# Loading turned decays, keys and queries as whole 128-row transfers, in a linear-attention and expert kernel

## The chip, the cores and the metric

The kernel runs on one core of a Trainium2 chip. The metric is the device time of one execution in microseconds, taken as the median of several runs; less is better. In the rows below, PE is the matrix engine (PEld its weight loads), DVE the vector engine, ACT the scalar engine, POOL the GpSimd engine and SP the queue that issues most transfers; L66 is the line of a helper through which every operation is recorded, so operations are told apart by their tiles.

## What is computed

Two stages. The first is a linear attention with a decaying state, over 4 batches, 8 heads, 768 steps and 48 channels:

```python
for t in range(S):
    state = alpha[:, :, t, :, None] * state + np.einsum('bhd,bhe->bhde', k[:, :, t], v[:, :, t])
    y[:, :, t] = np.einsum('bhd,bhde->bhe', q[:, :, t], state)
```

The second takes the 3072 rows of y (384 wide), picks for each row one of 8 experts by the largest gate logit, and computes `gate * (relu(x @ w1[e]) @ w2[e])` with an inner width of 1024.

## The kernel before

**Stages.** The attention works on 12 blocks (`PS`), here called pairs: a pair is 128 time steps of two batches with all 8 heads of each. Time runs along the free dimension. A head's 48 channels lie on partitions, and two heads share the 128 partitions: one on partitions 0 to 47, one on 64 to 111. Partitions 48 to 63 and 112 to 127 hold nothing that the result needs. Each of `X` (decays), `KT` and `QT` (keys, queries) holds 8 such double heads side by side (`KS = 8`), 4 of each half `z`. The host lays the inputs out in this shape with the unused rows already filled (`turned`: 1 for decays, 0 for keys and queries), so that the arrays in memory have all 128 rows.

For a pair, DVE scans the decays backward into `G` (`back`) and forward into `Fw` (`forth`), a half `z` at a time. POOL multiplies keys by `G` into `kh`; DVE or POOL multiplies queries by `Fw` into `qh`. PE forms the scores (`scores`), ACT copies them out as `scT`, POOL masks them (`causal`), PE multiplies them with the values `vt` (`from_values`) and adds the state's part (`from_state`). The finished rows `xs` are stored to memory by `store`. Pairs overlap: in step s of the loop, DVE scans pair s or s + 1 while PE handles the scores of pair s - 1.

Behind the attention the rows are routed, and 13 blocks of experts follow, in which PE multiplies almost without a pause.

**What sets the order.** Each engine keeps program order. SP issues the loads one after another: in front of the loop (lines 155 to 165) those of pair 0 in halves, those of pair 1 in halves with the values between, and the small gate weights `wgp`; in the loop the keys, queries and values of pair s + 1 at the head of step s (`load(s + 1, "kqv")`) and decays of a later pair at its end. There are 3 buffers for `X` and for `VT`, 2 for `KT` and `QT`.

**The lines that the change touches.** `load_turned` (lines 133 to 139) loads pair 0 over all 128 partitions, and every other pair as two transfers of 48 rows, one for each head of a double head. Because those transfers never write partitions 48 to 63 and 112 to 127, four ACT instructions (lines 157 to 160) fill the buffers that pair 0 does not use, once: `X[1]`, `KT[1]`, `QT[1]`, `X[2]`. Line 165 loads `wgp`.

Of the kernel before, what the change touches and what calls it, by code (L numbers as in the profile page):

```python
# [15 lines left out]
AF = mybir.ActivationFunctionType  # L16
# [5 lines left out]
P = 128  # L22
B, H, S, D = 4, 8, 768, 48
NC = S // P
NP = H // 2
SEG = P + 1
# [22 lines left out]
KS = 2 * NP  # L49
# [26 lines left out]
def attention_moe(ctx: ExitStack, tc: tile.TileContext, q, k, v, alpha, at_, kt_, qt_, vt_, mid, wg, wgp_, mb, w1, w2, out):  # L76
    nc = tc.nc
    order = [1]
    vec, act, pool, pe, sp = (Ordered(e, tc, order) for e in (nc.vector, nc.scalar, nc.gpsimd, nc.tensor, nc.sync))
# [6 lines left out]
    ident = cp.tile([P, P], F32, name="ident")  # L86
# [14 lines left out]
    NX_, NB, NV = 3, 2, 3  # L101
    KT = [ea.tile([P, KS, P], F32, name=f"kt{i}") for i in range(NB)]
    QT = [ea.tile([P, KS, P], F32, name=f"qt{i}") for i in range(NB)]
    X = [ea.tile([P, KS * SEG + 1], F32, name=f"X{i}") for i in range(NX_)]
# [25 lines left out]
    def small(p, *shape):  # L130
        return ps.tile([p, *shape], F32, name=next_bank())

    def load_turned(dst, src, s, z):
        if s == 0:
            sp.dma_start(dst[:, z], src[s, :, z])
        else:
            for g in range(2):
                r = slice(64 * g, 64 * g + D)
                sp.dma_start(dst[r, z], src[s, r, z])

    def load(s, names="akqv"):
        z = {"0": slice(0, NP), "1": slice(NP, KS)}.get(names[-1], slice(0, KS))
        for n in names:
            if n == "a":
                c = slice(z.start and z.start * SEG + 1, z.stop * SEG + 1)
                load_turned(X[s % NX_], at_, s, c)
            elif n in "kq":
                load_turned((KT if n == "k" else QT)[s % NB], kt_ if n == "k" else qt_, s, z)
            elif n == "v":
                sp.dma_start(VT[s % NV][:, : 2 * DM], vt_[s])  # L150

# [2 lines left out]
    wgp = cp.tile([P, NP, 32], F32, name="wgp")  # L154
    for n in "a0 k0 q0 a1 k1 q1".split():
        load(0, n)
    for t, x in ((X[1], 1.0), (KT[1], 0.0), (QT[1], 0.0), (X[2], 1.0)):
        n = KS * SEG + 1 if x else KS * P
        flat = t if x else t.rearrange("p k t -> p (k t)")
        act.activation(flat, ident[:, 0:1].broadcast_to([P, n]), AF.Copy, bias=x, scale=0.0)  # L160
    load(1, "a0")
    load(0, "v")
    for n in "k0 a1 q0 k1 q1 v".split():
        load(1, n)
    sp.dma_start(wgp, wgp_)


    room = ra.tile([P, 1024], F32, name="room")
# [37 lines left out]
    for i in range(2):  # L206
        t = ac.tile([P, KS, 64], F32, name=f"UB{i}")
# [55 lines left out]
    def back(s, z):  # L263
        x, G = X[s % NX_], st[s, "G"]
        r = slice(z.start * SEG + 1, z.stop * SEG + 1)
        vec.tensor_tensor_scan(G[:, r][:, ::-1], x[:, r][:, ::-1], DR[:, ::-1], 0.0, op0=ALU.mult, op1=ALU.max)

    def totals(s, z):
        r = slice(z.start * SEG + 1, z.stop * SEG + 1)
        vec.reciprocal(DF[:, 0::SEG], st[s, "G"][:, r][:, 0::SEG])  # L270

    def forth(s, z):
        f = slice(z.start * SEG, z.stop * SEG)
        vec.tensor_tensor_scan(st[s, "F"][:, f], X[s % NX_][:, f], DF, 0.0, op0=ALU.mult, op1=ALU.add)

    def scaled_keys(s, z, engine):
        engine.tensor_tensor(st[s, "k"][:, z], KT[s % NB][:, z], seg(st[s, "G"][:, 1:], 1, z), op=ALU.mult)

    def scaled_queries(s, z, engine=vec):
        engine.tensor_tensor(st[s, "q"][:, z], QT[s % NB][:, z], seg(st[s, "F"], 1, z), op=ALU.mult)  # L280

    def begin(s):
        st[s, "G"] = sb.tile([P, KS * SEG + 1], F32, name="G")
        st[s, "F"] = ea.tile([P, KS * SEG], F32, name="Fw", bufs=1)
        st[s, "k"] = sb.tile([P, KS, P], F32, name="kh")
        st[s, "q"] = sb.tile([P, KS, P], F32, name="qh")
# [7 lines left out]
    def scores(s, z):  # L294
        kh, qh = st[s, "k"], st[s, "q"]
        pp = [bank(NP, P) for _ in range(2)]
        for j in range(NP):
            for g in range(2):
                r = slice(64 * g, 64 * g + D)
                pe.matmul(pp[g][:, j], kh[r, NP * z + j], qh[r, NP * z + j], start=True, stop=True)  # L300
        sc = sb.tile([P, 2, NP, P], F32, name="scT", bufs=3)
        for g in range(2):
            act.copy(sc[:, g], pp[g])
        st[s, "s", z] = sc
        causal(s, z)
# [10 lines left out]
    def turn_keys(s, z):  # L316
        if z == 0:
            st[s, "n"] = sb.tile([P, 2, NP, P], F32, name="knat", bufs=1)
        p = bank(NP, P)
        for j in range(NP):  # L320
            pe.transpose(p[:, j], st[s, "k"][:, NP * z + j], ident)
        act.copy(st[s, "n"][:, z], p)
# [49 lines left out]
    def state(s):  # L372
        if s % NC > 0:
            S1 = sb.tile([P, KS, D], F32, name="S")
            kv = st[s - 1, "kv"]
            if s % NC > 1:
                vec.tensor_tensor(S1, UB[(s - 1) % 2][:, :, :D], kv, op=ALU.add)
            else:
                vec.tensor_copy(S1, kv)
            st[s, "S"] = S1  # L380
# [16 lines left out]
    def outputs(s, zs=(0, 1)):  # L397
        if 0 in zs:
            st[s, "yt"] = sb.tile([P, 2, NP, P], F32, name="yt")
        for z in zs:  # L400
            act.copy(st[s, "yt"][:, z], st[s, "yp"][z])
# [552 lines left out]
    def warm(n):  # L954
        w = bank(NP, P)
        for i in range(n):
            pe.matmul(w[:, i % NP], ident, ident, start=True, stop=True)

    for s in range(PS):
        if 0 < s and s + 1 < PS:  # L960
            load(s + 1, "kqv")
        if 0 <= s - 2:
            outputs(s - 2)
        late, by = [], vec
        if s == 0:
            warm(14)
            begin(0)
            for z in ZS:
                back(0, z)
                scaled_keys(0, z, pool)  # L970
                totals(0, z)
                forth(0, z)
                scaled_queries(0, z, pool if z == Z0 else vec)
        elif s == 1:
            begin(1)
            scores(0, 0)
            for z in range(2):
                turn_keys(0, z)
                if z == 0:
                    warm(2)  # L980
            back(1, Z0)
            scaled_keys(1, Z0, pool)
            scores(0, 1)
            totals(1, Z0)
            forth(1, Z0)
            scaled_queries(1, Z0, pool)
            back(1, Z1)
            scaled_keys(1, Z1, pool)
            totals(1, Z1)
            forth(1, Z1)  # L990
            scaled_queries(1, Z1)
        else:
            if (s - 1, "S") not in st:
                state(s - 1)
            decayed(s - 1)
            run(s, "state")
            for z in range(2):
                scores(s - 1, z)
            run(s, "masks")
            todo = scans(s)  # L1000
            if len(todo) > 1:
                late = todo.pop()
            if s >= 4:
                by = pool
            for f in todo:
                do(f)
            run(s, "counts")
        if 1 < s:
            keys(s - 1)
        if 0 <= s - 2:  # L1010
            rows(s - 2)
        if 0 <= 2 * (s - 3) < TURNED:
            turn_logits(s - 3)
        if 0 <= s - 2:
            logits_turned(s - 2)
        run(s, "small")
        if 0 <= 2 * (s - 3) < TURNED:
            sum_logits(s - 3)
        run(s, "middle")
        do(late[:-1])  # L1020
        if 0 <= s - 1:
            from_state(s - 1)
        if 0 <= s - 1 and (s - 1) % NC == 0:
            states(s - 1)
        if TURNED <= 2 * (s - 2):
            add_logits(s - 2)
        if 0 <= s - 1 and (s - 1) % NC:
            states(s - 1)
        run(s, "sums")
        for f, *x in late[-1:]:  # L1030
            f(*x, by)
        if 0 <= s - 1:
            from_values(s - 1)
        run(s, "end")
        for c in range(s - (s < 5), s + 1 - (s < 4)):
            if 0 <= c < PS:
                guard(c)
        if 0 <= s - 2:
            store(s - 2)
        for c in range(s + 2 + (s > 4), s + 3 + (s > 3)):  # L1040
            if c < PS:
                load(c, "a")
        if s == 1:
            sp.dma_start(mi.rearrange("p t w -> p (t w)"), mid.bitcast(I32))
            sp.dma_start(mbb, mb.unsqueeze(0).broadcast_to([P, NM, E]))
        if s == 2:
            sp.dma_start(xd[MID : MID + 1], of[0:1])
            sp.dma_start(gd[MID : MID + 1], of[0:1, 0:1])
# [54 lines left out]
    t = GROUPS[-2:]  # L1103
# [204 lines left out]
    for u in range(2):  # L1308
        us = slice(u * P, (u + 1) * P)
        op = py.tile([P, 512], F32, name=f"y{u}")[:, :DM]  # L1310
        for f in range(NF):
            j, z = divmod(f, 2)
# [110 lines left out]
```

## Time and profile before

| what | value |
|---|---|
| median of 3 runs | 348.19 us (347.65 to 348.42) |
| the profiled execution | 347.23 us |
| its span, first to last instruction | 345.5 us |
| PE busy | 334.1 us, 97% |
| DVE busy | 267.2 us, 77% |
| ACT busy | 234.3 us, 68% |
| POOL busy | 170.3 us, 49% |
| moved by DMA | 75.74 MB, mean 219 GB/s |

The profile is of one execution. Its own time is 1.73 us more than its span. A busy share is an average over stages with different limits, so it doesn't tell what a change in one stage is worth; the windows and timelines of that stage do. In a timeline, the bracket at a row's end is the time that the engine stood idle before it and what ended that time.

### The profile page before, as it was taken

What the parts mean: (1) busy time and instruction counts of PE and PEld (TensorE: products, weight loads), DVE (VectorE), ACT (ScalarE), POOL (GpSimd) and SP (SyncE); (2) the same over time, 40 slices, a digit from 0 to 9 for tenths busy, and PEclk for the clock granted to TensorE, in tenths of its full rate; (3) what the DMA queues carried; (4) which work ended last, traced back from release to release, by engine and by line L of the source; (5) the groups of instructions that cost most, each with busy time, mean ns of one, the idle gap of its engine ahead of it and who ended that gap; (6) DMA issues with size and microseconds to landing.
All of it is one profiled execution on the core that took longest, in us unless ns stands there. A gap on an engine that the chain in (4) does not pass through costs nothing. (4 is left out here: it accounts for less than half of the span.)

```text
span 345.5 us, 8427 instructions
## 1 busy us (share of the span) xinstructions
PE 334.1 (97%) x3162; PEld 303.7 (88%) x3162; DVE 267.2 (77%) x487; ACT 234.3 (68%) x458; POOL 170.3 (49%) x185
## 2 busy tenths in 40 slices
PE   8898999999999999999999999999999999999992
PEld 8787888888888886898989898989898989898992
DVE  7969999999995868786868686969696969696630
ACT  6766787767686524777777777777676767676540
POOL 8767689789668126556352424241254342411031
PEclk9998999999999999999999999999999999999997
DMA  7899999999455893998767667676586777670001
GB/s 236 234 235 276 289 222 237 249 258 260 140 183 187 290 341 84 367 383 283 260 217 237 242 208 246 208 250 207 188 259 232 230 243 210 244 224 25 2 25 56
DMA packets 39224, 75.74 MB, mean 219 GB/s; under 512 B 4443, under 2 KB 20980, under 8 KB 39172
## 3 DMA queue, kind: packets, MB, share of 16 engines
q1 hardware_dynamic: 35076, 65.05, 62.6%
q0 software_dynamic: 4096, 10.05, 8.7%
q8 instruction: 27, 0.44, 0.6%
q14 instruction: 25, 0.20, 0.2%
HBM read 65.43 MB, written 9.65 MB: 217 GB/s over the span
## 5 line engine op out<-in xcount | busy, mean ns | idle before, releaser
L66 PE MATMUL b<-xHL,w1H 128*128 128x512 f32 (+1 forms) x312 | 102.6, 378 | 0.5 <-ACT yt L66 0.5
L66 POOL DMA_INDIRECT out_dram<-os,idx x25 | 27.5, 1099 | 110.3 <-ACT os L66 65.3
L66 PE MATMUL b<-xHL,w1L 128*128 128x256 f32 x288 | 80.6, 280 | 0.0
L66 PEld LDWEIGHTS b<-xHL,w1H 128*128 128x128 f32 x312 | 57.4, 188 | 11.9 <-ACT yt L66 0.6
L66 PE MATMUL y<-w2H,hH 128*128 128x384 f32 x184 | 62.6, 340 | 0.0
L66 PE MATMUL y<-w2H,hL 128*128 128x384 f32 x184 | 61.7, 335 | 0.0
L66 PE MATMUL y<-w2L,hH 128*128 128x384 f32 x184 | 61.6, 335 | 0.0
L66 DVE TENSOR_TENSOR hs<-b,low 128x256 f32<-128x256 f32 x88 | 33.9, 414 | 32.7 <-ACT low L66 28.7
L66 PEld LDWEIGHTS b<-xHL,w1L 128*128 128x128 f32 x288 | 54.2, 188 | 0.1
L66 DVE TENSOR_TENSOR w1L<-w1r,w1H 128x768 fp32r<-128x768 f32 x48 | 43.8, 951 | 6.3 <-ACT w1H L66 6.3
L66 DVE TENSOR_TENSOR w2L<-w2r,w2H 128x768 fp32r<-128x768 f32 x48 | 45.8, 958 | 3.4 <-ACT w2H L66 3.4
L66 ACT ACTIVATE os<-y,gg 128x384 f32<-128x384 f32 x25 | 14.6, 584 | 39.6 <-PE y L66 37.5
L66 ACT CAST w2H<-w2r 128x768 fp32r<-128x768 f32 x48 | 40.1, 842 | 0.0
L66 ACT COPY low<-b 128x256 f32<-128x256 f32 x88 | 30.1, 368 | 14.5 <-PE b L66 13.0
L66 POOL DMA_INDIRECT xg<-xd,idx x26 | 29.6, 1138 | 20.8 <-DVE idx L66 11.6
L66 ACT CAST w1H<-w1r 128x768 fp32r<-128x768 f32 x48 | 37.9, 839 | 0.6 <-ACT ls L66 0.6
L66 POOL DMA_INDIRECT gg<-gd,idx x26 | 28.7, 1105 | 17.1 <-issue 13.4
L66 PEld LDWEIGHTS y<-w2L,hH 128*128 128x128 f32 x184 | 34.6, 188 | 0.0
L66 PEld LDWEIGHTS y<-w2H,hH 128*128 128x128 f32 x184 | 34.6, 188 | 0.0
L66 PEld LDWEIGHTS y<-w2H,hL 128*128 128x128 f32 x184 | 34.5, 188 | 0.0
L66 POOL TENSOR_TENSOR kh<-kt,G 128x512 f32<-128x512 f32 x24 | 28.8, 1206 | 10.7 <-DVE G L66 3.5
L66 ACT ACTIVATE hH<-hs 128x512 fp32r<-128x512 f32 x44 | 27.9, 634 | 7.6 <-DVE hs L66 6.1
(183 smaller groups left out, 602.7 us busy)
## 6 DMA issues: line engine op xcount, KB each, us to landing
w1r<-in_w_dram SPq DMA_DIRECT2D x26, 768.0 KB, 5.8
w2r<-in_w_dram SPq DMA_DIRECT2D x26, 768.0 KB, 5.2
vt<-in_paired_v_dram SPq DMA_DIRECT2D x12, 384.0 KB
xd<-xs SPq DMA_DIRECT2D x12, 384.0 KB, 4.6
X<-in_turned_alpha_dram SPq DMA_DIRECT2D x20, 193.7 KB, 6.3
kt<-in_turned_k_dram SPq DMA_DIRECT2D x20, 192.0 KB, 4.7
qt<-in_turned_q_dram SPq DMA_DIRECT2D x20, 192.0 KB, 7.6
kt<-in_turned_k_dram SPq DMA_DIRECT2D x2, 256.0 KB
```

The costliest lines, as they stand in the source:

```text
L66: ins = f(*a, **kw)
```

## The change

Every load of decays, keys and queries becomes one transfer over all 128 partitions, the unused rows included, as pair 0's already were. `load_turned` goes. The four fills on ACT go, since each load now writes the unused rows too. The load of `wgp` moves from the front of the loop to the end of step 0, behind the load of pair 2's decays.

```diff
-    def load_turned(dst, src, s, z):
-        if s == 0:
-            sp.dma_start(dst[:, z], src[s, :, z])
-        else:
-            for g in range(2):
-                r = slice(64 * g, 64 * g + D)
-                sp.dma_start(dst[r, z], src[s, r, z])
-
     def load(s, names="akqv"):
         z = {"0": slice(0, NP), "1": slice(NP, KS)}.get(names[-1], slice(0, KS))
         for n in names:
             if n == "a":
                 c = slice(z.start and z.start * SEG + 1, z.stop * SEG + 1)
-                load_turned(X[s % NX_], at_, s, c)
+                sp.dma_start(X[s % NX_][:, c], at_[s, :, c])
             elif n in "kq":
-                load_turned((KT if n == "k" else QT)[s % NB], kt_ if n == "k" else qt_, s, z)
+                sp.dma_start((KT if n == "k" else QT)[s % NB][:, z], (kt_ if n == "k" else qt_)[s, :, z])
             elif n == "v":
                 sp.dma_start(VT[s % NV][:, : 2 * DM], vt_[s])
...
     for n in "a0 k0 q0 a1 k1 q1".split():
         load(0, n)
-    for t, x in ((X[1], 1.0), (KT[1], 0.0), (QT[1], 0.0), (X[2], 1.0)):
-        n = KS * SEG + 1 if x else KS * P
-        flat = t if x else t.rearrange("p k t -> p (k t)")
-        act.activation(flat, ident[:, 0:1].broadcast_to([P, n]), AF.Copy, bias=x, scale=0.0)
     load(1, "a0")
     load(0, "v")
     for n in "k0 a1 q0 k1 q1 v".split():
         load(1, n)
-    sp.dma_start(wgp, wgp_)
...
             if c < PS:
                 load(c, "a")
+        if s == 0:
+            sp.dma_start(wgp, wgp_)
         if s == 1:
```

How this moves SP's instructions at the start of the program, as one piece of the difference (`X_86` to `X_88` are the three buffers of the decays, `kt_` and `qt_` those of keys and queries, `vt_` the values; the last number is the row length in words):

```order
-L66 DMA X_87<-in_turned_alpha_dram 48x517 x2
+L66 DMA X_87<-in_turned_alpha_dram 128x517
 L66 DMA vt_89<-in_paired_v_dram 128x768
-L66 DMA kt_83<-in_turned_k_dram 48x512 x2
-L66 DMA X_87<-in_turned_alpha_dram 48x516 x2
-L66 DMA qt_85<-in_turned_q_dram 48x512 x2
-L66 DMA kt_83<-in_turned_k_dram 48x512 x2
-L66 DMA qt_85<-in_turned_q_dram 48x512 x2
+L66 DMA kt_83<-in_turned_k_dram 128x512
+L66 DMA X_87<-in_turned_alpha_dram 128x516
+L66 DMA qt_85<-in_turned_q_dram 128x512
+L66 DMA kt_83<-in_turned_k_dram 128x512
```

Two transfers of 48 rows become one of 128 in the same place; nothing else changes its place there but `wgp`.

SP's next instructions in before, with the semaphores that each waits for (`DMAHW0` to `DMAHW7` are eight semaphores that transfers use in turn, so a transfer waits for the eighth one before it to land; the other names are engines that release a buffer):

```order
L66 DMA vt_90<-in_paired_v_dram 128x768 [waits DMAHW3_49]
L66 DMA wgp<-in_wgp_dram 128x128 [waits DMAHW4_49]
L66 DMA X_88<-in_turned_alpha_dram 48x1033 [waits DMAHW5_49,Activation_49]
L66 DMA X_88<-in_turned_alpha_dram 48x1033 [waits DMAHW6_49]
L66 DMA kt_82<-in_turned_k_dram 48x1024 [waits DMAHW7_49,Pool_49]
L66 DMA kt_82<-in_turned_k_dram 48x1024 [waits DMAHW0_49]
L66 DMA qt_84<-in_turned_q_dram 48x1024 [waits DMAHW1_49,DVE_49]
L66 DMA qt_84<-in_turned_q_dram 48x1024 [waits DMAHW2_49]
```

and the same place in the changed kernel:

```order
L66 DMA vt_90<-in_paired_v_dram 128x768 [waits DMAHW5_49]
L66 DMA X_88<-in_turned_alpha_dram 128x1033 [waits DMAHW6_49]
L66 DMA wgp<-in_wgp_dram 128x128 [waits DMAHW7_49]
L66 DMA kt_82<-in_turned_k_dram 128x1024 [waits DMAHW0_49,Pool_49]
L66 DMA qt_84<-in_turned_q_dram 128x1024 [waits DMAHW1_49,DVE_49]
```

The load of pair 2's decays stands ahead of `wgp` now and no longer waits for ACT's fill; all of SP's instructions until the program's end go from 640 to 604. On ACT the four fills are gone from the head of the queue; PE, DVE and POOL have the same instructions in the same order.

## Rows read from the trace of the kernel before

**Rows 1.** The page's head and its line of busy times, whole program.

```profile
span 345.5 us, 8427 instructions
...
PE 334.1 (97%) x3162; PEld 303.7 (88%) x3162; DVE 267.2 (77%) x487; ACT 234.3 (68%) x458; POOL 170.3 (49%) x185
```

**Rows 2.** Windows: length; busy PE, PEld, DVE, ACT, POOL; granted clock, DMA share, GB/s.

```profile
28.00:29.00 1.00, 1.00 (x9) 0.78 (x8) 0.93 (x3) 0.39 (x1) 1.00 (x2) 0.50 1.01 264
50.00:60.00 10.00, 10.00 (x202) 8.74 (x194) 9.38 (x14) 7.46 (x17) 10.00 (x10) 1.00 1.05 233
```

**Rows 3.** Timeline of PE, 12 to 60 us: start, length, operation, [idle before].

```profile
14.09 1.09 PE L66 MATMUL b<-scT,vt 128*64 128x128 f32 x16 [0.84 <-POOL scT L66]
...
17.03 1.16 PE L66 MATMUL b<-qh,kh 48*128 48x128 f32 x16 [0.63 <-DVE qh L66]
...
20.02 0.64 PE L66 MATMUL b<-yt,wgp 128*32 128x256 f32 x8
...
24.45 1.16 PE L66 MATMUL b<-qh,kh 48*128 48x128 f32 x16
27.01 1.57 PE L66 MATMUL b<-qh,kh 48*128 48x128 f32 x16 [1.39 <-DVE qh L66]
...
36.26 2.06 PE L66 MATMUL b<-qh,kh 48*128 48x128 f32 x32
...
44.83 2.06 PE L66 MATMUL b<-qh,kh 48*128 48x128 f32 x32
```

**Rows 4.** Timeline of POOL, 11 to 36 us.

```profile
11.79 1.19 POOL L66 TENSOR_TENSOR kh<-kt,G 128x512 f32<-128x512 f32 x1 [0.84 <-DMA kt<-in_turned_k_dram]
12.95 1.09 POOL L66 TENSOR_SCALAR_AFFINE_SELECT scT<-scT 128x1024 f32<-128x1024 f32 x1
...
15.16 1.18 POOL L66 TENSOR_TENSOR kh<-kt,G 128x512 f32<-128x512 f32 x1
...
32.44 2.35 POOL L66 TENSOR_TENSOR kh<-kt,G 128x512 f32<-128x512 f32 x2
```

**Rows 5.** Timeline of DVE, 14 to 36 us.

```profile
15.46 1.42 DVE L66 TENSOR_TENSOR qh<-qt,Fw 128x512 f32<-128x512 f32 x1 [0.18 <-DMA qt<-in_turned_q_dram]
...
19.27 1.23 DVE L66 TENSOR_TENSOR_SCAN G<-X,room 128x516 f32<-128x516 f32 x1 [1.92 <-DMA X<-in_turned_alpha_dram]
...
22.82 0.69 DVE L66 TENSOR_TENSOR qh<-qt,Fw 128x512 f32<-128x512 f32 x1 [0.77 <-DMA qt<-in_turned_q_dram]
...
26.17 0.69 DVE L66 TENSOR_TENSOR qh<-qt,Fw 128x512 f32<-128x512 f32 x1
...
34.95 0.69 DVE L66 TENSOR_TENSOR qh<-qt,Fw 128x512 f32<-128x512 f32 x1
```

**Rows 6.** Windows (columns as in rows 2), read for the last two columns.

```profile
2.00:6.00 4.00, 4.00 (x20) 4.00 (x20) 3.16 (x8) 3.99 (x5) 3.63 (x15) 1.00 0.98 303
11.00:12.00 1.00, 1.00 (x32) 0.88 (x30) 0.86 (x3) 0.70 (x2) 0.21 (x1) 1.00 0.81 201
57.00:58.00 1.00, 1.00 (x36) 0.81 (x32) 1.00 (x2) 1.00 (x4) 1.00 (x2) 1.00 1.07 197
62.00:63.00 1.00, 1.00 (x12) 0.89 (x9) 0.93 (x3) 1.00 (x3) 0.55 (x1) 1.00 1.11 416
150.00:160.00 10.00, 10.00 (x59) 9.50 (x59) 5.99 (x9) 6.05 (x11) 3.73 (x4) 1.00 1.05 386
```

**Rows 7.** The page's DMA issues: count, KB of each, us to landing.

```profile
vt<-in_paired_v_dram SPq DMA_DIRECT2D x12, 384.0 KB
...
X<-in_turned_alpha_dram SPq DMA_DIRECT2D x20, 193.7 KB, 6.3
kt<-in_turned_k_dram SPq DMA_DIRECT2D x20, 192.0 KB, 4.7
```

**Rows 8.** Timeline of ACT, 1 to 13 us.

```profile
8.68 1.07 ACT L66 COPY scT<-b 128x512 f32<-128x512 f32 x2 [2.67 <-PE b L66]
...
11.30 1.07 ACT L66 COPY scT<-b 128x512 f32<-128x512 f32 x2 [0.56 <-PE b L66]
```

## The prediction

> **What bounds the kernel now.** I read the page's busy line first, then the windows, then the timelines of PE, DVE and POOL where PE stands still, then the DMA rate of single stretches. PE is busy 334.1 us of a span of 345.5 us [rows 1]. From the fourth pair on it does not pause: between 50 and 60 us it is busy for all 10.00 us, DVE for 9.38 us [rows 2], and the scores of two neighbouring pairs start at 36.26 and 44.83 us with no idle time noted in between, 8.57 us a pair [rows 3]. A microsecond in the attention loop is therefore worth something only if it lets PE start that unbroken run earlier, or run it faster.
>
> Ahead of the run PE stands still at three places [rows 3]: 0.84 us before 14.09 (for POOL's masked scores), 0.63 us before 17.03 (for a query product on DVE) and 1.39 us before 27.01 (for a query product on DVE). [...] From the second half of one pair's scores to the first half of the next takes 36.26 - 27.01 = 9.25 us there. [...]
>
> Two of the three halts lead back to a transfer. Before 14.09: POOL waited 0.84 us for `kt`, then did `kh` (1.19 us) and only then the mask [rows 4]. Before 27.01: DVE waited 1.92 us for `X` at 19.27 and 0.77 us for `qt` at 22.82, and ran without a further wait up to the query product at 26.17 [rows 5].
>
> The transfers are late because the DMA engines are full (share 1.05 from 50 to 60 us [rows 2]) at a low rate: 197 GB/s where the 48-row loads pass, against 416 GB/s between them and 386 GB/s in the weight loads [rows 6].
>
> **The change, part by part.**
>
> *Bytes and rate.* Six 48-row loads of a pair, 2 x (193.7 + 192 + 192) = 1155 KB [rows 7], become three of 128 rows: 516.5 + 512 + 512 = 1540.5 KB, a third more. `vt` (384 KB [rows 7]) and the store of `xs` (384 KB by its shape) stay. In before, 1.18 MB at 197 GB/s take 6.0 us and the other 0.79 MB at 386 GB/s 2.0 us: 8.0 us of a PE step of 8.57 us. No 128-row load with rows of 4 KB is in the trace. Bounds: 197 GB/s, if long rows are what is slow; 416 GB/s, the best stretch. I take 386, since the 48-row loads are slow with short rows too: the first ones, with 2 KB rows, show 201 GB/s at a share of 0.81 from 11 to 12 us, so 248 at a full one, against 303 for the 128-row loads of 2 KB rows from 2 to 6 us [rows 6]. Then 1.58 MB take 4.1 us, and the step's transfers 6.1 us. The DMA engines stop being full.
>
> *Is X of pair 2 on time?* The queue ahead of it, and with it, holds 1540.5 KB each of pairs 0 and 1, two `vt` of 384 KB and its own 516.5 KB: 4365.5 KB, 4.47 MB. At 303 GB/s, the mean of the first loads (128 rows throughout) from 2 to 6 us [rows 6], it ends at 2.0 + 14.8 = 16.8 us; at 386 GB/s at 13.6. DVE could begin at 17.35 (19.27 - 1.92). It comes in time at both ends. DVE's chain from there to the query product's end is 26.86 - 19.27 - 0.77 = 6.82 us, so it is ready at 24.2 or earlier; PE arrives at 25.0 (below). X may land 0.8 us late before PE sees it.
>
> *`kt` of pair 1, first half*: 2.50 MB with what stands ahead; at 303 GB/s 10.2 us, at 386 8.5 us. POOL is free for it at 11.79 - 0.84 = 10.95 us [rows 4]. The mask behind can't start before ACT has copied the scores, 11.30 + 1.07 = 12.37 us [rows 8], so it gains 12.95 - 12.38 = 0.57 us at most, and does so if `kt` lands by 11.2 us.
>
> *The halts.* Mask 0.57 us earlier: PE's 14.09 becomes 13.52. All of POOL's queue behind moves with it, so the next `kh` (15.16 to 16.34) ends at 15.77. The query product at 15.46 lasts 1.42 us, against 0.69 us for the same operation at 22.82 and 26.17 [rows 5]; it runs beside that `kh` and ends 0.54 us after it [rows 4, 5]. If it stays behind `kh`, it ends 0.57 us earlier; if it were free of it, at 15.28 + 0.69 = 15.97, 0.91 us earlier. I take the first, by the row. [...] So PE's 17.03 becomes 16.46, the halt before it as long as it was, and PE reaches the end of the next half scores (24.45 + 1.16 = 25.61) at 25.04. The query product is there at 24.2, so the 1.39 us go whole. Sum: 0.57 + 1.39 = **1.96 us**.
>
> *The clock.* With those 1.39 us gone no pause is left right ahead of the slow stretch. The halts of 0.84 and 0.63 us were not followed by a slow one. I expect the clock to stay up: **1.68 us**; the other end is 0.
>
> *What is late next.* PE would ask for the second half of pair 3's scores at 37.25 - 3.64 = 33.6. DVE's query product for it ends at 35.64 [rows 5], 2.69 us (1.92 + 0.77) earlier 32.95: in time by 0.65 us. POOL's two `kh` end at 34.79 [rows 4]; the mask ahead of them waits for ACT and so follows PE, and they end near 32.4. No new halt, but little room.
>
> *At nothing.* The four ACT fills: ACT stands idle 2.67 us behind them [rows 8]. SP issues 36 transfers fewer (640 - 604 rows of its order); each waits for the eighth one before it to land (the order rows), so those in flight hold more than twice the bytes. The 64 KB of `wgp` now stand behind X of pair 2 and are first used at 20.02 us [rows 3]; by the sum above they land near 17.0 at the slow end. If `wgp` were late, PE would wait there one for one.
>
> **Sum.** 1.96 + 1.68 = 3.64 us of the profiled execution's 347.23 us. The median of the runs is 348.19, 0.96 us above it; I set the same 3.64 off against the median: **344.6 us**.
>
> **The rivals.**
>
> 1. *The waits go, the clock still falls* (here or a little later; the start of PE's work is as ragged as before). 348.19 - 1.96 = 346.2 us. For it: 0.63 us of halt remain at 16.5. Against: the row of the half clock follows the longest halt.
>
> 2. *Long rows are slow, whatever the partitions.* Then 1.58 MB at 197 GB/s take 8.0 us, with 2.0 us for the rest 10.0 us a pair against PE's 8.57: 1.4 us for each of nine pairs, +13 us less what is gained, near 359 us. It decides from 1.58 / (8.57 - 2.0) = 240 GB/s down. For it: every 4 KB load shown is slow. Against: the 248 GB/s of the 2 KB loads of 48 rows (above). [...]
>
> 3. *Another wait takes the place.* DVE is at 9.38 of 10 us [rows 2]; if DVE or POOL can't keep the earlier pace (the 0.65 us above), PE halts at pair 3 or 4 for about what it gained: 347.6 to 348.6 us, no change.
>
> [...]
>
> **How the numbers follow.** Forecast (344.6) 0.48; rival 1 0.27; rival 3 0.12; rival 2 and other losses, such as `kt` or `wgp` late at the start by over a microsecond, 0.06; rival 4 0.07. The range takes rivals 1 and 4 in, and half a microsecond on either side of them for the step from one execution to a median: 343.3 to 347.2. A measurement of this kernel tells about 0.2%, 0.7 us, from no change. Faster than 347.5: 0.48 + 0.27 + 0.07 and a little of rival 3, 0.84; same 0.10; slower 0.06.
>
> **What would show it.** Right: no wait of DVE for `X` and of POOL for `kt` in the list of waits; DMA share of a late attention window near 0.75, with no 197 GB/s stretch; PE without idle time from about 16.5 us; pair 3's scores (now 36.26) at about 32.6 with the clock full, 34.3 with the slow stretch. Wrong: 197 GB/s stretches that stay, new waits of PE for DVE or POOL between 25 and 45 us, or a span shorter by less than the shift of pair 3's scores, which would mean that the stage of the experts gives it back.

## The result and the profile after

The changed kernel takes **343.96 us** (median of 6 runs, 343.68 to 344.31). The kernel before, on the same chip, takes 348.56 us (6 runs, 347.65 to 351.53). The ratio is 0.9853, 95% interval 0.9815 to 0.9891. (Ratios here leave out runs more than 1.5% above the fastest of their kernel, and need not be the quotients of the medians.) The forecast was 344.6 us with a range of 343.3 to 347.2. The two profiled executions differ less than the medians: 347.23 before, 343.79 after, so 3.44 us.

The page of the changed kernel, its head and its line of busy times, against [rows 1]: the span is 3.4 us shorter, and PE's busy time fell by 3.3 us. PE does the same 3162 multiplications; it runs none of them at the half clock now (granted 1.00 in every stretch from 0 to 338 us; before, 0.50 from 28 to 31 us), which is worth 1.61 to 1.68 us (below), about half of the 3.3 us. In a second profiled execution of each kernel PE's busy time fell by 1.5 us (333.8 to 332.3). ACT has lost its four fills (458 instructions became 454).

```profile
span 342.1 us, 8364 instructions
...
PE 330.8 (97%) x3162; PEld 300.7 (88%) x3162; DVE 265.7 (78%) x487; ACT 229.5 (67%) x454; POOL 170.8 (50%) x185
```

The timeline of PE in the changed kernel, with the operations of [rows 3]:

```profile
13.90 1.09 PE L66 MATMUL b<-scT,vt 128*64 128x128 f32 x16 [0.34 <-POOL scT L66]
15.06 1.16 PE L66 MATMUL b<-qh,kh 48*128 48x128 f32 x16
16.84 1.16 PE L66 MATMUL b<-qh,kh 48*128 48x128 f32 x16 [0.62 <-DVE qh L66]
...
24.27 2.06 PE L66 MATMUL b<-qh,kh 48*128 48x128 f32 x32
...
32.84 2.06 PE L66 MATMUL b<-qh,kh 48*128 48x128 f32 x32
...
41.41 2.06 PE L66 MATMUL b<-qh,kh 48*128 48x128 f32 x32
```

The scores of pair 2 are one row now (24.27, 32 multiplications): the halt of 1.39 us between their halves is gone. Pair 3's scores start at 32.84 where they started at 36.26, so 3.42 us earlier; 32.6 was predicted. From pair 2 on a step is 8.57 us.

Windows of the changed kernel, columns as in [rows 2]; they answer to [rows 2, 6]:

```profile
11.00:12.00 1.00, 1.00 (x28) 0.88 (x25) 0.86 (x3) 0.39 (x1) 0.74 (x2) 1.00 1.04 385
28.00:29.00 1.00, 1.00 (x17) 0.42 (x16) 0.85 (x3) 1.00 (x4) 1.00 (x1) 1.00 1.03 407
50.00:60.00 10.00, 10.00 (x160) 8.84 (x159) 9.56 (x13) 8.13 (x18) 10.00 (x10) 1.00 0.93 315
57.00:58.00 1.00, 1.00 (x22) 1.00 (x21) 1.00 (x2) 0.46 (x2) 1.00 (x2) 1.00 0.83 232
```

At 28 to 29 us the granted clock is 1.00, where it was 0.50. From 11 to 12 us the transfers run at 385 GB/s instead of 201. Between 50 and 60 us the DMA engines move 315 GB/s at a share of 0.93; before it was 233 GB/s at 1.05. More bytes pass and less of the engines' time goes. The 232 GB/s from 57 to 58 us stand beside a share of 0.83, so they are partly a lack of work.

The timeline of DVE at the start, against [rows 5]:

```profile
6.86 1.23 DVE L66 TENSOR_TENSOR_SCAN G<-X,room 128x516 f32<-128x516 f32 x1 [0.71 <-DMA X<-in_turned_alpha_dram]
...
10.22 1.22 DVE L66 TENSOR_TENSOR_SCAN G<-X,room 128x516 f32<-128x516 f32 x1
...
15.63 1.06 DVE L66 TENSOR_TENSOR qh<-qt,Fw 128x512 f32<-128x512 f32 x1
16.62 0.55 DVE L66 COPY S<-kv 128x384 f32<-128x384 f32 x1
17.09 1.21 DVE L66 TENSOR_TENSOR_SCAN G<-X,room 128x516 f32<-128x516 f32 x1
...
23.56 0.69 DVE L66 TENSOR_TENSOR qh<-qt,Fw 128x512 f32<-128x512 f32 x1
```

And that of POOL, against [rows 4]:

```profile
11.52 1.20 POOL L66 TENSOR_TENSOR kh<-kt,G 128x512 f32<-128x512 f32 x1 [0.26 <-DVE G L66]
12.76 1.09 POOL L66 TENSOR_SCALAR_AFFINE_SELECT scT<-scT 128x1024 f32<-128x1024 f32 x1
...
14.97 1.17 POOL L66 TENSOR_TENSOR kh<-kt,G 128x512 f32<-128x512 f32 x1
```

The waits of DVE for `X` (1.92) and `qt` (0.77) and of POOL for `kt` (0.84) are gone behind pair 0. The wait for the second half of pair 0's own `X` is longer (0.71). DVE begins pair 2's scan at 17.09, 2.18 us earlier, and has the query product at 24.25; the mask of POOL is only 0.19 us earlier. SP issues pair 2's `X` at 9.10 us instead of 14.40. In the timeline of SP before:

```profile
14.40 0.84 SPq L66 DMA_DIRECT2D X<-in_turned_alpha_dram  x2
```

and after:

```profile
9.10 0.33 SPq L66 DMA_DIRECT2D X<-in_turned_alpha_dram  x1
```

So this load lands earlier for two reasons that come together: the transfers ahead of it pass faster (385 GB/s from 11 to 12 us instead of 201), and there are fewer of them to wait for (pair 1 comes in 6 loads instead of 12; with 12 loads over all 128 partitions, the column halves below, SP issues it at 12.33 us).

### The profile page after: what moved, and what is told of

It is laid out like the page before. It is cut to its first block, busy times and chain, and to the rows that moved or that the text cites. A ratio compares the mean times of both kernels' runs of the same rounds, so it can differ in the third digit from the quotient of the medians.

```text
span 342.1 us, 8364 instructions
## 1 busy us (share of the span) xinstructions
PE 330.8 (97%) x3162; PEld 300.7 (88%) x3162; DVE 265.7 (78%) x487; ACT 229.5 (67%) x454; POOL 170.8 (50%) x185
## 5 line engine op out<-in xcount | busy, mean ns | idle before, releaser
L66 DVE TENSOR_TENSOR hs<-b,low 128x256 f32<-128x256 f32 x88 | 33.9, 415 | 32.6 <-ACT low L66 32.6
L66 ACT COPY scT<-b 128x512 f32<-128x512 f32 x48 | 24.8, 599 | 14.2 <-PE b L66 13.1
L66 POOL TENSOR_TENSOR kh<-kt,G 128x512 f32<-128x512 f32 x24 | 30.5, 1278 | 6.3 <-DVE G L66 5.7
```

The costliest lines, as they stand in the source:

```text
L66: ins = f(*a, **kw)
```

## The experiments

Most of them cut the loads of pairs 1 to 11 in another way. The kernel before ran beside each batch on that batch's chip: 348.32 us median (345.02 to 350.53, 23 runs) for the first four, 347.92 (345.06 to 352.74, 26 runs) for the next four, 348.76 (345.58 to 352.11, 23 runs) for the next three. Its runs spread over 5.5 to 7.7 us; those of the changed kernel over 0.6 and, when it ran again, 2.2 us.

**All rows, but in two transfers of 64** (the changed kernel, with this for the loads of pairs 1 to 11; the rest of the edit is left out here).

```diff
+            for g in range(2):
+                r = slice(64 * g, 64 * g + 64)
+                sp.dma_start(dst[r, z], src[s, r, z])
```

> The changed kernel, but each load of pairs 1 to 11 in two transfers of 64 rows (partitions 0 to 63, then 64 to 127): the same bytes as the changed kernel, as many transfers as before. Theory A (a transfer that stays within one half of the partitions runs at half the rate): 197 GB/s in these loads, so 1.58 MB take 8.0 us and a pair's transfers 10.0 us against the 8.57 us of PE; the attention becomes bound by transfers, waits of DVE for X and POOL for kt in most pairs, and the time is 9 to 14 us longer than before, 356 to 362 us. Theory B (fewer instructions in flight, no fills, wgp moved): the number of transfers is that of before, so the gain of the transfers goes, the time is near before's, 347 to 349 us, with the 197 GB/s stretches lasting a third longer. Theory C (whole rows give the gain by their alignment or length): as fast as the changed kernel, 344 us.

Measured: 357.99 us (357.62 to 361.05, 4 runs), ratio 1.0309 (1.0247 to 1.0371). The same bytes as in the changed kernel, 14 us slower, and within the range of theory A. Its list of waits (us in total, times, longest):

```profile
DVE qh L66 <- DMA qt<-in_turned_q_dram: 8.8, 6, 2.3
POOL qh L66 <- DMA qt<-in_turned_q_dram: 5.0, 4, 1.5
POOL kh L66 <- DMA kt<-in_turned_k_dram: 3.1, 2, 2.0
```

Two rows of its PE timeline, halts that go on far into the attention:

```profile
29.83 1.16 PE L66 MATMUL b<-qh,kh 48*128 48x128 f32 x16 [2.18 <-DVE qh L66]
...
65.67 1.98 PE L66 MATMUL b<-qh,UB 64*64 64x128 f32 x32 [3.47 <-POOL UB L66]
```

Rows, their length and the bytes are those of the changed kernel; only the cut differs. So it is not the reading of unused rows that helps, nor their length that harms. The time is that of rival 2, from another cause: the DMA engines, at a share of 1.03 to 1.07 from 20 to 60 us, move 227 to 273 GB/s and can't keep up with a pair per 8.57 us.

**One transfer of 112 rows** (partitions 0 to 111, the kernel before otherwise, fills kept).

```diff
-            for g in range(2):
-                r = slice(64 * g, 64 * g + D)
-                sp.dma_start(dst[r, z], src[s, r, z])
+            r = slice(0, 64 + D)
+            sp.dma_start(dst[r, z], src[s, r, z])
```

> Before with one transfer of 112 rows (partitions 0 to 111) for each load of pairs 1 to 11, the fills kept: an eighth fewer bytes than the changed kernel, both halves of the partitions reached, as few transfers. Theory A (what counts is that one transfer reaches both halves): most of the gain, 343.8 to 345.5 us, the DMA share of a late attention window under 1. Rival (what counts is the full 128 rows, evenly spread over the DMA engines): rates near those of 48 rows, 347 us or more.

Measured: 351.12 us (346.61 to 352.51, 12 runs), ratio 1.005 (1.0009 to 1.0091): slower than before. One transfer that reaches both halves is not enough: theory A fell. Its window from 50 to 60 us shows a full DMA and a PE that is not:

```profile
50.00:60.00 10.00, 9.61 (x168) 7.75 (x166) 8.84 (x13) 7.21 (x17) 8.32 (x9) 1.00 1.03 299
```

**All 128 rows, in two transfers by columns** (the changed kernel, each load of pairs 1 to 11 cut in the free dimension; the two lines that use it are left out here).

```diff
+    def load_turned(dst, src, s, z):
+        h = (z.start or 0) + (z.stop - (z.start or 0)) // 2
+        parts = [z] if s == 0 else [slice(z.start, h), slice(h, z.stop)]
+        for c in parts:
+            sp.dma_start(dst[:, c], src[s, :, c])
```

> The changed kernel, but every load of X, kt and qt of pairs 1 to 11 is split in two by columns: each transfer still covers all 128 partitions, with rows of half the length (1 or 2 KB). Refined theory (what counts is that one transfer covers all 128 rows evenly; the run of 112 rows and the run of two times 64 rows each lack that): about the changed kernel, 343.5 to 345.5 us, 128-row stretches near 400 GB/s, no new wait of DVE for qt. Rival (what made the two times 64 rows slow was twice the number of transfers, with half the bytes in flight when each waits for the eighth ahead of it): slow like that run, 350 to 360 us, waits of DVE for qt of 2 us and more.

Measured: 344.51 us (343.24 to 346.22, 6 runs), ratio 0.9879 (0.983 to 0.9928), as the changed kernel. The rival fell. Twice the transfers cost nothing that the median shows, but something in the trace: SP issues pair 2's `X` at 12.33 us instead of 9.10, and DVE waits for it again. Its list of waits has this row, whose longest wait, 1.3 us, is that of pair 2 (the other two are pair 0's):

```profile
DVE G L66 <- DMA X<-in_turned_alpha_dram: 3.2, 3, 1.3
```

PE does not halt for it, and pair 3's scores start at 33.79 us instead of 32.84. What these three runs leave standing is that for the gain every transfer here has to cover all 128 partitions; fewer transfers bring the first loads sooner, which by itself is worth less than the runs can tell.

The page's DMA queues say the same in bytes and engine time. The hardware queue of the kernel before (packets, MB, share of the 16 engines' span):

```profile
q1 hardware_dynamic: 35076, 65.05, 62.6%
```

Of the changed kernel:

```profile
q1 hardware_dynamic: 35652, 69.38, 58.8%
```

Of the run with two times 64 rows:

```profile
q1 hardware_dynamic: 36228, 69.38, 64.8%
```

Of the run with 112 rows:

```profile
q1 hardware_dynamic: 35076, 67.21, 62.0%
```

Of the run with column halves:

```profile
q1 hardware_dynamic: 40836, 69.38, 60.0%
```

Share times span (345.5, 342.1, 355.9, 349.3, 342.5 us) is 216, 201, 231, 217 and 206 us of all 16 engines, so 301, 345, 301, 310 and 338 GB/s while they work, with the same weights among the bytes in all. The changed kernel moves 4.3 MB more in 15 us less.

So two transfers, one on each half of the partitions, bring 301 GB/s and one of 112 rows 310, where transfers over all 128 bring 338 and 345. No view here shows which engine writes which rows, so why the two halves and the 112 rows are slow stays open.

**Only X, or only kt and qt, as 128 rows** (the kernel before otherwise).

```diff
-        if s == 0:
+        if s == 0 or dst.shape[1] == KS * SEG + 1:
```

> The kernel before, with only X loaded over 128 partitions in one transfer; kt and qt stay two times 48 rows. Proportional theory (each narrow load takes the DMA engines' time, and the gain is in the sum): 516.5 + 768 KB at 386 GB/s and 768 KB at 197 GB/s make 3.4 + 4.0 = 7.4 us of a pair's 8.57, against 8.0 before and 6.1 after, so a third of the gain: 346 to 347.5 us. Rival (X of pair 2, the longest wait of DVE, is what matters, and it is now one wide load): 344 to 345.5 us, no wait of DVE for X behind pair 1.

> The kernel before, with only kt and qt loaded over 128 partitions in one transfer each; X stays two times 48 rows. Proportional theory: 1024 + 768 KB at 386 GB/s and 387 KB at 197 GB/s make 4.75 + 2.0 = 6.75 us of a pair's 8.57, two thirds of the gain or more: 344 to 345.5 us. Rival (X of pair 2 is what matters, and it is still narrow): 346 to 347.5 us, with a wait of DVE for X of a microsecond or more ahead of pair 2.

Measured: X alone 349.35 us (345.56 to 351.04, 12 runs), ratio 0.9994 (0.9953 to 1.0036), no gain; kt and qt alone (the test is `KS` then) 346.22 us (344.69 to 349.04, 12 runs), ratio 0.9958 (0.992 to 0.9996), some 2.5 us of medians. By the ratio the gain of kt and qt alone is 0.4%, some 1.5 us, with an interval that ends just short of no change. The rival (X of pair 2 alone matters) fell. The proportional theory has the order right and both sizes too good. The profiled execution with X alone is the slowest of its twelve (351.04 us), so it is read for its single waits only. DVE waits for `X` of pair 2 in spite of the wide load, and longer than before for `qt`:

```profile
DVE G L66 <- DMA X<-in_turned_alpha_dram: 3.1, 3, 1.4
DVE qh L66 <- DMA qt<-in_turned_q_dram: 1.4, 1, 1.4
```

The longest wait for `X` is pair 2's. Together the two waits of pair 2 are 1.41 + 1.37 = 2.78 us, where they were 1.92 + 0.77 = 2.69 [rows 5]. That the narrow `kt` and `qt` around it hold up a wide `X`, because they share the DMA engines, fits but is not shown. In the trace with kt and qt alone DVE waits 0.57 us for pair 2's `X` and not for `qt`, and PE's third halt is gone.

**Only pairs 1 and 2, or only pairs 3 to 11, as 128 rows** (the condition `s == 0` becomes `s <= 2`, or `s == 0 or s > 2`).

> Before, with the loads of pairs 1 and 2 alone as 128-row transfers; fills and wgp as in before, pairs 3 to 11 in two of 48 rows. Theory A (all of the gain comes from pairs 1 and 2 being on time and the clock that stays up): within 0.8 us of the changed kernel, 343.7 to 344.8 us, PE's first scores of pair 3 near 32.8 us, no half clock, while 197 GB/s stretches stay in the later pairs. Rival (the relief of the transfers in all pairs matters): clearly above, 346 us or more, with new waits for X, kt or qt of pairs 3 and 4.

> Before, with pairs 3 to 11 as 128-row transfers and pairs 1 and 2 in two of 48 rows as before. Theory A: the halts of PE before 14.09, 17.03 and 27.01 us stay, and so does the slow clock behind them where it comes: 347.5 to 349 us, no change from before that can be told, though the DMA share of a late attention window falls from 1.05 to 0.9. Rival (all pairs): faster than before by 1 us or more.

Measured: the early pairs alone 344.53 us (343.35 to 346.66, 6 runs), ratio 0.9887 (0.9846 to 0.9928); the late pairs alone 346.55 us (343.58 to 348.13, 12 runs), ratio 0.9972 (0.9937 to 1.0007). Nearly the whole gain is made by the loads of two pairs, ahead of PE's unbroken run, as the prediction's reading had it. The late pairs' interval takes in no change, but the median lies 1.8 us lower (1.0 us by the ratio), lower than I had expected of them: that is left unexplained, and a gain of a microsecond from the later loads is not ruled out. Pair 3's scores in the profiled executions, first of the early pairs alone (346.66 us, the slowest of its six), then of the late pairs alone (343.58, the fastest of its twelve):

```profile
33.30 2.32 PE L66 MATMUL b<-qh,kh 48*128 48x128 f32 x32
```

```profile
33.82 2.06 PE L66 MATMUL b<-qh,kh 48*128 48x128 f32 x32
```

The early pairs alone have neither the third halt nor a half clock in the attention (pair 2's scores to pair 3's take 8.94 us, where the kernel before took 11.81), as theory A said, but a new wait of DVE of 1.20 us for pair 2's `qt`, and pair 3's scores start at 33.30, not near 32.8. With the late pairs alone DVE started pair 2's scan at 18.79 us instead of 19.27 [rows 5]; PE halted 0.81 and 0.63 us at the first two places, as before, and not at the third. So even with narrow early loads an execution can escape the third halt.

**The halt kept busy** (the kernel before, with 10 unused multiplications of `ident`, 20 in the trace, between the halves of pair 2's scores, and a bank of PSUM for them).

```diff
+                if s == 3 and z == 0:
+                    warm(10)
```

> Before, with ten extra multiplications of the identity into a spare bank between the two halves of pair 2's scores, where PE stands still for 1.39 us; their result is not used, and all transfers stay late. Theory A, its clock part (the half clock follows from PE standing still there): the granted clock stays full behind 27 us, the step from pair 2's second half of scores to pair 3's first takes 7.6 us in place of 9.25, and the time is 1.2 to 1.7 us less than before, near 347 us. Rival (the clock falls from something else, the start of the program for one): no change, 348.2 to 348.8 us, the half clock at the same place.

Measured: 349.37 us (347.7 to 352.06, 12 runs), ratio 1.0027 (0.9995 to 1.006), no gain. Its PE timeline says why:

```profile
25.47 2.50 PE L66 MATMUL b<-ident 128*128 128x128 f32 x20
27.90 1.16 PE L66 MATMUL b<-qh,kh 48*128 48x128 f32 x16
...
35.54 1.72 PE L66 MATMUL b<-qh,kh 48*128 48x128 f32 x26
```

The step from 27.90 to 35.54 is 7.64 us instead of 9.25: the clock stayed up (1.00 from 28 to 29 us), and its price is 1.61 us. But the added work takes 2.50 us, and PE reaches the second half at 27.90, behind DVE's query product (26.58) and 0.89 us later than before. Of the difference, 0.72 us, 0.29 are left at the last scores (104.87 against 105.16 us), and none in the time of the twelve runs. That it was the added work that kept the clock up is not shown: in the run with X alone the clock stayed up behind a halt of 1.50 us (last section).

**The fills and the old place of `wgp` put back** into the changed kernel, and, also in the changed kernel, **X's second half third** in pair 0 (`a0 k0 a1 q0 k1 q1`).

> All loads of 128 rows as in the changed kernel, but the four ACT fills are back and wgp is loaded at its old place. Theory A (the rows of the transfers are all of it): the same as the changed kernel within 0.3 us. Rival (the fills or wgp's place carry some of the gain): 0.5 us or more above it, with a wait of SP for the fills before the first loads of pair 1.

> The changed kernel with the second half of pair 0's decays loaded third in place of fourth, ahead of the first half of its queries. In the changed kernel DVE waits 0.7 us for it near 6.9 us and POOL is free for the queries earlier. If the start of DVE's chain is what is left of the late transfers: PE's first scores of pair 3 up to 0.6 us earlier, 343.4 to 343.9 us. If the queries, now late, or ACT's copies take the place: no change from the changed kernel.

Measured: with fills 344.21 us (343.83 to 345.41, 7 runs), ratio 0.9895 (0.9854 to 0.9936), against 344.53 us (343.66 to 345.81, 8 runs), ratio 0.9909 (0.9876 to 0.9942), of the changed kernel run again beside it; its expectation:

> The changed kernel once more, for the spread of its runs beside those of before on one chip. Theory A: with no transfer that arrives at the last moment, and the clock up in every run, its runs lie close together, within about 1 us around 344, where 23 runs of before spread over 345.0 to 350.5 us. Rival (the spread belongs to the chip or to the experts' stage): a spread of 3 us or more, around 344.

The changed kernel's runs spread over 2.2 us, between the 1 us of theory A and the 3 us of the rival. The four fills and the place of `wgp` carry nothing that these runs can tell. The other order gave 345.12 us (342.99 to 347.71, 12 runs), ratio 0.993 (0.99 to 0.9959): no better, and more scattered. No version tried is clearly faster than the changed kernel.

**The kernel before once more.**

> The kernel before once more, for a second profiled execution (the first took 347.23 us, with pair 3's scores starting at 36.26 us). Theory (the spread of this kernel's runs, 345 to 352 us, comes from when the narrow loads of pairs 1 to 3 land, ahead of PE's unbroken run): the start of pair 3's second pair of scores (44.83 us in the first execution) differs from the first execution by about as much as the time does, within 1 us, and X or qt wait by another amount. Rival (the spread arises in the stage of the experts or at the end): the scores of pair 3 and 4 start within 0.5 us of 36.26 and 44.83, and the difference is behind 114 us.

Measured: 348.1 us (346.67 to 349.93, 8 runs); the profiled execution took 346.85. Its PE timeline:

```profile
27.26 1.37 PE L66 MATMUL b<-qh,kh 48*128 48x128 f32 x16 [1.94 <-DVE qh L66]
...
36.51 2.06 PE L66 MATMUL b<-qh,kh 48*128 48x128 f32 x32
```

Its DVE timeline:

```profile
19.40 1.23 DVE L66 TENSOR_TENSOR_SCAN G<-X,room 128x516 f32<-128x516 f32 x1 [2.34 <-DMA X<-in_turned_alpha_dram]
```

Its window behind the halt, columns as in [rows 2]:

```profile
28.00:29.00 1.00, 1.00 (x10) 0.78 (x8) 0.93 (x3) 0.35 (x1) 1.00 (x2) 0.53 0.98 208
```

The mechanism repeats, step for step: late `X`, halt, half clock, 9.25 us. On the spread it decides nothing, because this execution took nearly the time of the first: 45.08 against 44.83 us fits both theories.

## Why the prediction was right

*The waits, 1.96 us predicted, 1.74 seen.* With its second half taken as 1.0 us into the row at 24.27, as the prediction did for pair 4, pair 2's second half of scores starts at 25.27 instead of 27.01. The third halt went whole, and it was worth more than the 1.39 us of its row: before, the second half started 27.01 - 24.45 = 2.56 us behind the first, 1.56 more than the 1.0 without a halt. The first term, 0.57 us from an earlier mask, gave 0.19: POOL did stop waiting for `kt`, but DVE's scans of pair 0 began later. In the second pair of profiled executions it gave nothing: there POOL did not wait for that `kt` in the kernel before either, and PE's masked scores start at 13.78 us before and 14.12 after; the third halt was 1.94 us there, and the sum 1.78. Two rows of the kernel before's DVE timeline, to be set against those of after at 6.86 and 10.22:

```profile
6.55 1.23 DVE L66 TENSOR_TENSOR_SCAN G<-X,room 128x516 f32<-128x516 f32 x1 [0.38 <-DMA X<-in_turned_alpha_dram]
...
9.91 1.22 DVE L66 TENSOR_TENSOR_SCAN G<-X,room 128x516 f32<-128x516 f32 x1
```

0.31 us came in there, at the second half of pair 0's `X`. That load is the same in both kernels, but its wait follows the change: 0.33 to 0.41 us in the four traces whose pair 1 comes in 48-row loads throughout, 0.70 to 0.79 in the four whose pair 1 comes in whole 128-row ones (the changed kernel twice, the fills back, the early pairs alone). The prediction had put nothing down for what the wider loads behind take from pair 0's own; that they take it in the DMA engines is argued, not shown. ACT's copy of the scores, which was the floor of my term, moved from 11.30 to 11.61 with it. The halt ahead of 16.84 stayed as it was (0.62 for 0.63), which speaks for the row that I took: the query product that ran beside POOL's `kh` still ends half a microsecond behind it (16.69 against 16.14).

*The clock, 1.68 us predicted, 1.61 to 1.68 seen.* The term is 9.25 us less the 7.57 us of the next step at a granted clock of 1.00 (36 to 45 us), which is 44.83 - 36.26 = 8.57 us [rows 3] less 1.0 us, half of its first row (2.06). From pair 2's second half to pair 3's scores 9.25 us became 32.84 - 25.27 = 7.57. That uses the prediction's own 1.0 us for half a pair's scores; where the halves stand apart and the clock stays up, in the runs with X alone, with 112 rows and with the halt kept busy, the step is 7.64, so the clock's price is 1.61. Rival 1 did not occur in either profiled execution of the changed kernel (1.00 from 28 to 29 us in both).

*The transfers.* "The DMA engines stop being full" was too strong: the share from 50 to 60 us is 0.93, not the 0.7 of my sum (6.1 of 8.57 us); 0.73 comes only later, from 70 to 80 us. X of pair 2 was on time, and no long-row penalty showed (399 GB/s from 20 to 25 us, with 4 KB rows over 128 partitions among the loads). The sum went by bytes and rate; that SP now issues fewer transfers stood under *At nothing*, but SP issues this load 5.3 us earlier.

*What was late next.* Nothing: no halt at pair 3, as the 0.65 us of room had said. Rival 3 did not occur. The 0.9 us of rival 4, for which the 0.63 us halt would have had to go too, no run shows: the halt stayed, at 0.62 us in the changed kernel and 0.43 to 0.88 us in the others.

*Behind the attention.* The whole lead is carried to its end: the last scores start at 101.73 us instead of 105.16. The first expert block, in the kernel before:

```profile
114.23 0.39 PE L66 MATMUL b<-xHL,w1H 128*128 128x256 f32 x1 [0.54 <-ACT yt L66]
```

And in the changed kernel:

```profile
109.94 0.36 PE L66 MATMUL b<-xHL,w1H 128*128 128x256 f32 x1
```

From the last scores to it the kernel before took 9.07 us, the changed one 8.21. These 0.86 us are not the change's: the changed kernel's second profile has the same halt (0.54, for ACT's `yt`) and takes 9.48 us, and the second one of the kernel before has none and takes 8.20. From the first expert block to the last multiplication both take the same (224.4 us). Behind that, 0.96 us more pass in after than in before (7.81 against 6.85). So 3.42 + 0.86 - 0.96, and the span ends 3.4 us earlier: that the stage behind neither added nor took is chance. In the second pair of executions the lead is 3.46 us at pair 3's scores and 2.7 at the end.

*From one execution to the median.* I set the sum of one execution off against the median, and the sum fits the first pair of executions best (3.64 against 3.44; the second pair differs by 2.76). On the medians the gain was 4.6 us in the first comparison and 3.4 in the second. How a median's gain divides between waits and clock no run shows. The two profiled executions of the kernel before both have the slow stretch, and took 347.23 and 346.85 us, less than that kernel's medians. The mean granted clock of a run without a trace can't tell whether it had one, because the clock also stands at 0.50 behind the last multiplication, where it costs nothing: from 342 us to the end of the span in the kernel before, from 340 us in the changed one; the run with X alone has a mean of 0.993 without a slow stretch in the attention. So the mechanism came out as forecast, and that the median lies 0.6 us from the forecast is partly luck: the mask's term was too large, the halt's too small, and the step from an execution to a median (347.23 against 348.56 us before) is larger than the half microsecond that the range allowed. A comparison also tells less than the 0.2% that I took: the interval is 0.4% to either side.

## What to carry to other kernels

Load over all 128 partitions in each transfer, even where a quarter of the rows is never read: here a third more bytes of these loads took the DMA engines less time (201 us instead of 216, the weights' loads among it). Two transfers of 64 rows (231 us) or one of 112 (217 us) did not do it; cutting the columns (206 us) lost nothing in the median. And price a late load by what it starts: the wait before the unbroken run of the bounding engine counts once, and where the clock falls behind it (1.6 us here) about as much again.

## What was not expected of the hardware

*A halt does not settle the clock.* The halts of 1.39 and 1.94 us were followed by the half clock (0.50 and 0.53 from 28 to 29 us), and so were those of 1.69 us in the run with 112 rows (0.50 from 40 to 43 us) and of 2.18 us in that with two times 64 (a mean of 0.83 from 30 to 40 us); behind that run's 3.47 us 32 multiplications took 1.98 us that took 1.10 a pair earlier. The clock stayed up behind 1.13 us with 112 rows (1.00 from 27 to 29 us) and 1.17 us with two times 64 (1.00 from 50 to 60 us). In the run with X alone it also stayed up, behind a halt of 1.50 us (the step to pair 3 takes 34.96 - 27.32 = 7.64 us). Its PE timeline:

```profile
27.32 1.16 PE L66 MATMUL b<-qh,kh 48*128 48x128 f32 x16 [1.50 <-DVE qh L66]
```

Its window:

```profile
28.00:29.00 1.00, 1.00 (x14) 0.88 (x12) 0.96 (x2) 0.47 (x1) 1.00 (x2) 1.00 0.92 165
```

*PE halts that wait for no data.* In three kernels PE stops in the middle of a group of multiplications with "issue" as the releaser. The PE timeline of the run with 112 rows:

```profile
38.37 0.48 PE L66 MATMUL b<-qh,kh 48*128 48x128 f32 x2 [1.69 <-issue]
...
54.60 1.63 PE L66 MATMUL b<-scT,vt 128*64 128x128 f32 x25 [0.39 <-issue]
```

They stand behind the 472nd and the 725th multiplication. The run with X alone halts behind the 472nd too (0.64 us), that with the early pairs alone behind the 598th (0.51 us). The distances are 126 and 127 multiplications. In all three the DMA share stands above 1 around the first halt (1.03 from 35 to 38.3 us with 112 rows, 1.01 from 35 to 38 us with X alone, 1.04 from 36 to 43 us with the early pairs alone, against 0.80 from 31 to 38 us in the changed kernel). Whether the full DMA has a part in the halts was not tried by itself, and a full DMA alone does not bring them: the kernel before has no such halt at a share of 1.04 from 36 to 43 us, nor have the column halves at 0.99 (38 to 45 us). The cause stays open. In the run of 112 rows the halt of 1.69 us is followed by a clock of 0.50 from 40 to 43 us.
